# Where the constants lie: the fp32 identity behind the others, and kT tiles rounded up to 128 bytes

## The chip, the cores and the metric

The kernel runs on one core of a Trainium2 chip. The metric is the device time of one execution in microseconds, the lower the better. A kernel's time is the median of its runs; the profile comes from one further execution.

## The reference, cut to what matters

```python
# q, k, v: (8, 8, 576, 64) fp32;  w_in: (512, 2048);  w_out: (2048, 512)
scores = q @ k.T / 8                       # per batch and head, 576 x 576
rel = pos[:, None] - pos[None, :]
mask_local   = (rel >= 0) & (rel < 32)                 # heads 0 to 3
mask_strided = (rel >= 0) & (pos % 32 equal)           # heads 4 to 7
attn = softmax(where(mask, scores, -1e9))
x = (attn @ v) laid out as (4608 tokens, 512)
h = x @ w_in
out = where(h > 0, h, exp(min(h, 0)) - 1) @ w_out      # (4608, 512) fp32
```

So it is a sparse attention (a band of 32 keys for half of the heads, every 32nd key for the other half), followed by a two-layer network with an ELU between the layers.

## The kernel before

All data of a batch are brought in by DMAs that POOL issues and that turn fp32 into bf16 on the way. Strided heads are laid out so that partition p holds eight neighbouring positions, local heads in blocks of 96 or 128 positions. The attention of a batch works on four pairs of heads ("s0", "s1" strided, "l0", "l1" local), each in two halves: scores on PE (`scores`, L457), exponentials on ACT (`exp_s`, L464), the mask on DVE (`mask`, L471 and L477), the product with v on PE (`pv`, L484 to L527), then log, exponential and a product on ACT and DVE that put the normalised result into `xT`. The network works on nine chunks of 512 tokens: `l1` (L612) makes 16 groups of 128 hidden units, `exp_h`, `clamp` and `elu` (L620 to L640) apply the ELU and write the result into `g`, `l2` (L646) multiplies by `w_out_sb`, a copy (L652) brings the result into `osb`, and `store` (L664) writes it to HBM. The last group is cut into pieces (L676, L686).

The order of everything is written out by hand in one long list, ORDER, which every engine follows in its own queue: `w` is a matmul on zeros that only keeps PE going, `T` and `c` transpose q and k on PE and copy them out, `D` issues a load, `X` a DMA transpose, `S e m O n r x` are the steps of the attention and `a b L h i j g Z q o t` those of the network. Batches 0 and 1 are transposed on PE; from batch 2 on `dma_T` (L605) has SP's queue transpose the raw tiles into `qT` and `kT`. Loads to the raw tiles `qs`, `ks`, `vs` are runs of 512 bf16; `load_qloc` (L244), `load_kloc` (L251) and `load_vloc` (L261, L263) write pieces of 64 bf16, since two heads are woven into one row or a row of ones stands between two pieces of v. The weights come in eight loads, four to `w_in_sb` (L276) and four to `w_out_sb` (L280).

All tiles that live through the whole kernel come from one pool, `consts`, which lays them one behind another in the order in which they are named, each at the next multiple of 32 bytes of a partition. The order is: xT, g0, g1, w_in_sb, w_out_sb, zero, identity, identity_f, ones, the raw tiles qs, ks, ql, kl, vs, ql1, kl1, then vl0, vl1, vsp, the four qT, the four kT (s0, l0, s1, l1), and dist, same, eq, mask_s, mask_1, mask_l. Behind them come the pools of e, pm, ln, he, he1 and osb. `identity_f` is the fp32 identity with which the first q and k, staged in `g[0]` as fp32, are transposed (L405); it is written by one memset on DVE (L307) and one select on POOL (L312). Batch 1 is loaded into parts of xT and g[1] instead of the raw tiles.

```python
identity = consts.tile([128, 128], BF16, tag="identity", name="identity")
identity_f = consts.tile([RS, RS], F32, tag="identity_f", name="identity_f")   # RS = 72
ones = consts.tile([128, D], BF16, tag="ones", name="ones")
KSW = 2 * NS * RP + 128 - RP       # 1328 bf16 = 2656 bytes
KLW = PRE + 2 * S                  # 1184 bf16 = 2368 bytes
```

Of the kernel before, what the change touches and what calls it, by code (L numbers as in the profile page):

```python
# [8 lines left out]
F32 = mybir.dt.float32  # L9
BF16 = mybir.dt.bfloat16  # L10
# [6 lines left out]
D = 64  # L17
HG = 4
NS = 8
RS = S // NS  # L20
RP = 80
LQ = 96
LB = S // LQ
LN = LQ // NS
PRE = STRIDE
# [124 lines left out]
def kernel(  # L150
# [18 lines left out]
    consts = ctx.enter_context(tc.tile_pool(name="consts", bufs=1))  # L169
# [13 lines left out]
    w_out_sb = consts.tile([128, MC, d_model], BF16, tag="w_out_sb", name="w_out_sb")  # L183
    zero = consts.tile([128, CHUNK], BF16, tag="zero", name="zero")
    identity = consts.tile([128, 128], BF16, tag="identity", name="identity")
    identity_f = consts.tile([RS, RS], F32, tag="identity_f", name="identity_f")
    ones = consts.tile([128, D], BF16, tag="ones", name="ones")


# [17 lines left out]
    KLW = PRE + 2 * S  # L207

    qT = [{c: consts.tile([128, 2 * NS * RP], BF16, tag=f"qT{c}{i}", name=f"qT{c}{i}")
           for c in "sl"} for i in range(2)]  # L210
    kT = [{c: consts.tile([128, n], BF16, tag=f"kT{c}{i}", name=f"kT{c}{i}")
           for c, n in (("s", KSW), ("l", KLW))} for i in range(2)]
    dist = consts.tile([RS, RS], I32, tag="dist", name="dist")
    same = consts.tile([RS, RS], I32, tag="same", name="same")
# [1 line left out]
    mask_s = consts.tile([RS, RS], BF16, tag="mask_s", name="mask_s")  # L216
    mask_1 = consts.tile([128, NS, LN], BF16, tag="mask_1", name="mask_1")
    mask_l = consts.tile([128, 2, NS, 3, LN], BF16, tag="mask_l", name="mask_l")

    def rawof(nm, b):  # L220
        if b == 1:
            return raw1[nm]
        return odd[nm] if b % 2 and nm in odd else raw[nm]

    def runs(x, b, h, n):

        rows = RP if (b * H + h + n - 1) * S + RP * NS <= B * H * S else RS
        return rows, bass.AP(x.tensor, x.offset + (b * H + h) * S * D,
                             [[NS * D, rows], [S * D, n], [1, NS * D]])
# [65 lines left out]
    for eng, n, x in ((nc.sync, 0, q), (nc.scalar, 1, k)):  # L295
        for i in range(2):
            rows, in_ = runs(x, 0, HG, 2)
            f = NS * D // 2
            eng.dma_start(out=half(stage[0:rows, n * 4 * f:(n + 1) * 4 * f], i),
                          in_=in_[:, :, i * f:(i + 1) * f])  # L300
# [12 lines left out]
        identity_f, identity_f, compare_op=ALU.is_equal, fill=0.0,  # L313
# [281 lines left out]
    def dma_T(what, b):  # L595
        nm, c = what
        n = HG * NS // 2
        t = (qT if nm == "q" else kT)[int(b) % 2][c]
        in_ = rawof(what, int(b))
        if what == "kl":  # L600
            t, in_ = t[:, PRE:], in_[:, 0:HG * LB * D]
        else:
            t = t[:, 0:n * RP]
        p = LQ if what == "kl" else RP
        nc.sync.dma_start_transpose(out=t.rearrange("c (n p) -> c n p", p=p), in_=in_)  # L605
# [75 lines left out]
    def out_piece(ch, kk, i):  # L681
# [11 lines left out]
        "C": lambda *a: copy_T(nc.scalar.copy, *a),  # L693
        "S": scores, "e": exp_s, "m": mask, "O": pv, "n": log_sums, "r": recip, "x": write_x,
        "V": copy_vloc, "W": copy_vstr, "D": load, "X": dma_T,
        "a": lambda ch, m, bk: l1(ch, m, (2, 3), bk), "b": lambda ch, m: l1(ch, m, (0, 1)),
        "L": lambda ch, m, bk: l1(ch, m, (2, 3, 0, 1), bk), "h": exp_h,
# [39 lines left out]
```

## Time and profile before

| | |
|---|---|
| median of 3 runs | 307.03 us (306.18 to 308.11) |
| profiled execution | 306.21 us, of which the span is 304.5 us |
| PE busy (matmul) | 297.1 us, 98% |
| ACT, DVE, POOL busy | 226.8, 225.5, 81.0 us |
| DMA packets | 107,358, 37.63 MB |
| POOL's DMA queue (q0) | 69,728 packets, 19.47 MB, 72.0% of 16 engines |
| HBM read, written | 39.53 MB, 9.44 MB |

A busy share is that of an engine's instructions; DMA-issuing instructions are not counted. Matmuls are pipelined and their ends are modelled, so the groups' mean durations (379 ns for a matmul of 512 columns) are longer than the distance from one start to the next. The share of a DMA queue adds up the times of its packets over 16 engines; packets in flight at the same time count twice, so it can be over 100% of a stretch.

### The profile page before, as it was taken

What the parts mean: (1) busy time and instruction counts of PE and PEld (TensorE: products, weight loads), DVE (VectorE), ACT (ScalarE), POOL (GpSimd) and SP (SyncE); (2) the same over time, 40 slices, a digit from 0 to 9 for tenths busy, and PEclk for the clock granted to TensorE, in tenths of its full rate; (3) what the DMA queues carried; (4) which work ended last, traced back from release to release, by engine and by line L of the source; (5) the groups of instructions that cost most, each with busy time, mean ns of one, the idle gap of its engine ahead of it and who ended that gap; (6) DMA issues with size and microseconds to landing.
All of it is one profiled execution on the core that took longest, in us unless ns stands there. A gap on an engine that the chain in (4) does not pass through costs nothing.

```text
span 304.5 us, 6251 instructions
## 1 busy us (share of the span) xinstructions
PE 297.1 (98%) x2336; PEld 147.1 (48%) x2336; DVE 225.5 (74%) x435; ACT 226.8 (74%) x409; POOL 81.0 (27%) x111
## 2 busy tenths in 40 slices
PE   7999999999999999999999999999999999999994
PEld 3654455445544454445544554445444544444444
DVE  6777868698789978896788878976788358895020
ACT  2878778598879888997989889978777569982101
POOL 8823436651085008521087350000000000000000
PEclk9999999999999999999999999999999999999999
DMA  7999999999999999999989999931120022000054
GB/s 164 178 205 207 206 193 158 142 184 171 201 137 139 195 155 143 142 185 161 194 145 159 62 144 110 209 72 56 38 69 0 2 69 69 2 1 0 4 152 123
DMA packets 107358, 37.63 MB, mean 124 GB/s; under 512 B 89152, under 2 KB 102848, under 8 KB 107328
## 3 DMA queue, kind: packets, MB, share of 16 engines
q0 software_dynamic: 69728, 19.47, 72.0%
q1 hardware_dynamic: 36920, 17.08, 30.8%
q10 hardware_dynamic: 680, 0.69, 0.8%
q8 instruction: 18, 0.29, 0.4%
q14 instruction: 12, 0.10, 0.1%
HBM read 39.53 MB, written 9.44 MB: 161 GB/s over the span
## 4 chain that ended last, share of the span: by engine, by line
PE 82%; DMA 13%; DVE 2%; POOL 1%; issue 1%; ACTq 0%; DVEq 0%
PE ps L646 38%; PE ps L612 35%; DMA w_out_sb<-in_moe_w_out_dram 6%; DMA w_in_sb<-in_moe_w_in_dram 5%; PE ps L457 3%; PE ps L527 2%; PE ps L520 2%; DMA g<-in_k_dram 2%; PE ps L676 1%; DVE g L640 1%; POOL w_in_sb L276 1%; POOL vl L261 0%; DVE he L629 0%; DVE xT L585 0%; POOL xT L234 0%
## 5 line engine op out<-in xcount | busy, mean ns | idle before, releaser
L646 PE MATMUL ps<-w_out_sb,g 128*128 128x512 bf16 x560 | 132.8, 379 | 1.0 <-DVE g L640 0.5
L612 PE MATMUL ps<-xT,w_in_sb 128*128 128x512 bf16 x576 | 130.5, 379 | 0.1
L620 ACT ACTIVATE he<-ps 128x512 f32<-128x512 f32 x144 | 80.9, 597 | 22.0 <-PE ps L612 20.1
L612 PEld LDWEIGHTS <-w_in_sb 128*128 128x128 bf16 x576 | 54.9, 98 | 64.4 <-issue 1.2
L646 PEld LDWEIGHTS <-g 128*128 128x128 bf16 x560 | 51.2, 97 | 56.2 <-issue 1.1
L640 DVE TENSOR_TENSOR g<-he,ps 128x512 bf16<-128x512 bf16 x92 | 62.0, 684 | 1.9
L585 DVE TENSOR_TENSOR xT<-ps,ln 64x576 bf16<-64x576 f32 (+1 forms) x64 | 42.6, 678 | 20.1 <-ACT ln L560 19.1
L464 ACT ACTIVATE e<-ps 72x576 bf16<-72x576 f32 (+1 forms) x64 | 39.1, 647 | 15.6 <-PE ps L457 14.5
L629 DVE TENSOR_SCALAR he<-he 128x512 bf16<-128x512 f32 x92 | 39.2, 435 | 7.8 <-ACT he L620 7.4
L555 ACT ACTIVATE ln<-ps 64x576 f32<-64x576 f32 (+1 forms) x64 | 36.2, 583 | 10.0 <-PE ps L527 4.9
L638 DVE SCALAR_TENSOR_TENSOR g<-he,ps 128x512 bf16<-128x512 bf16 x52 | 34.8, 683 | 7.2 <-ACT he L627 6.7
L560 ACT ACTIVATE ln<-ln 64x576 f32<-64x576 f32 (+1 forms) x64 | 38.5, 619 | 1.2
L627 ACT ACTIVATE he<-he 128x512 bf16<-128x512 f32 x52 | 32.5, 630 | 1.0 <-DVE g L640 0.6
L652 DVE COPY osb<-ps 128x512 f32<-128x512 f32 x22 | 15.1, 685 | 16.8 <-PE ps L646 16.5
L244 POOL DMA_DIRECT2D ql<-in_q_dram x24 | 20.4, 855 | 10.5 <-DMA vl<-in_v_dram 5.7
L251 POOL DMA_DIRECT2D kl<-in_k_dram x24 | 17.9, 751 | 15.2 <-DMA w_out_sb<-in_moe_w_out_dram 4.5
L652 ACT COPY osb<-ps 128x512 f32<-128x512 f32 x13 | 7.6, 586 | 17.9 <-PE ps L646 14.1
L477 DVE TENSOR_TENSOR pm<-e,mask_l 128x576 bf16<-128x576 bf16 x32 | 14.1, 454 | 7.0 <-ACT e L464 5.4
L471 DVE TENSOR_TENSOR pm<-e,mask_s 72x576 bf16<-72x576 bf16 x32 | 14.2, 450 | 4.4 <-ACT e L464 4.2
L520 PEld LDWEIGHTS <-vsp 72*128 72x128 bf16 x192 | 9.1, 98 | 5.5 <-DVE pm L471 0.3
L261 POOL DMA_DIRECT2D vl<-in_v_dram x8 | 9.8, 1230 | 7.1 <-PE ps L527 4.9
L234 POOL DMA_DIRECT2D vs<-in_v_dram x8 | 5.2, 650 | 21.1 <-DVE vsp L592 17.8
(90 smaller groups left out, 152.2 us busy)
## 6 DMA issues: line engine op xcount, KB each, us to landing
out_dram<-osb SPq DMA_DIRECT2D x30, 144.0 KB
vl<-in_v_dram POOLq DMA_DIRECT2D x8, 288.0 KB, 9.9
w_in_sb<-in_moe_w_in_dram POOLq DMA_DIRECT2D x4, 512.0 KB, 13.7
w_out_sb<-in_moe_w_out_dram POOLq DMA_DIRECT2D x4, 512.0 KB, 17.4
kl<-in_k_dram POOLq DMA_DIRECT2D x24, 72.0 KB, 8.6
ql<-in_q_dram POOLq DMA_DIRECT2D x24, 72.0 KB, 8.5
ks<-in_k_dram POOLq DMA_DIRECT2D x5, 320.0 KB, 9.2
vs<-in_v_dram POOLq DMA_DIRECT2D x5, 320.0 KB, 9.6
```

Of the source, the lines that this page charges most:

```text
L464: nc.scalar.activation(e[0:R], tiles.pop(("S", key, u))[0:R], ACT.Exp, scale=scale)
L555: nc.scalar.activation(t, s_ps, ACT.Ln)
L560: nc.scalar.activation(t, t, ACT.Exp, scale=-1.0)
L585: nc.vector.tensor_mul(dst, o_ps, rc)
L612: nc.tensor.matmul(tiles["h", ch, m], lhsT=w_in_sb[:, c, m * 128:(m + 1) * 128], rhs=xT[:, c, ch * CHUNK:(ch + 1) * CHUNK], start=(c == 2) ...
L620: nc.scalar.activation(e, tiles["h", i[0], i[1]], ACT.Exp)
L627: nc.scalar.activation(e1, e, ACT.Relu, bias=1.0, scale=-1.0)
L629: eng.tensor_scalar(e1, e, scalar1=1.0, scalar2=1.0, op0=ALU.min, op1=ALU.subtract)
L638: nc.vector.scalar_tensor_tensor(dst, e1, -1.0, h, op0=ALU.mult, op1=ALU.max)
L640: nc.vector.tensor_tensor(dst, e1, h, op=ALU.max)
L646: nc.tensor.matmul(ops, lhsT=g[ch % 2][:, m, kk * 128:(kk + 1) * 128], rhs=w_out_sb[:, m, :], start=(m == 0), stop=(m == MC - 1), skip_gro ...
L652: eng(o_sb, tiles.pop(("o", int(ch), int(kk))))
```

## The change

identity_f is allocated last instead of between identity and ones, with a row of 80 instead of 72 fp32 (320 instead of 288 bytes), of which the first 72 are used. The kT tiles are rounded up to a multiple of 64 bf16: 1344 instead of 1328 (2688 bytes) and 1216 instead of 1184 (2432 bytes). The transpose into kTl names its end, KLW, since the tile is now longer. With that, ones and all tiles that DMAs write start at multiples of 128 bytes. No instruction is added, removed or moved; two clears of kTs are 8 words longer.

```diff
     identity = consts.tile([128, 128], BF16, tag="identity", name="identity")
-    identity_f = consts.tile([RS, RS], F32, tag="identity_f", name="identity_f")
     ones = consts.tile([128, D], BF16, tag="ones", name="ones")
...
-    kT = [{c: consts.tile([128, n], BF16, tag=f"kT{c}{i}", name=f"kT{c}{i}")
+    kT = [{c: consts.tile([128, -(-n // 64) * 64], BF16, tag=f"kT{c}{i}", name=f"kT{c}{i}")
            for c, n in (("s", KSW), ("l", KLW))} for i in range(2)]
...
     mask_l = consts.tile([128, 2, NS, 3, LN], BF16, tag="mask_l", name="mask_l")
+    identity_f = consts.tile([RS, RP], F32, tag="identity_f", name="identity_f")[:, 0:RS]
...
         if what == "kl":
-            t, in_ = t[:, PRE:], in_[:, 0:HG * LB * D]
+            t, in_ = t[:, PRE:KLW], in_[:, 0:HG * LB * D]
```

## The prediction

> **What bounds the kernel now.** I read the page first: which engine fills the span, how full the DMA engines are, and what the throttle grants.
>
> ```profile
> span 304.5 us, 6251 instructions
> ...
> PE 297.1 (98%) x2336; PEld 147.1 (48%) x2336; DVE 225.5 (74%) x435; ACT 226.8 (74%) x409; POOL 81.0 (27%) x111
> ...
> PEclk9999999999999999999999999999999999999999
> DMA  7999999999999999999989999931120022000054
> ...
> q0 software_dynamic: 69728, 19.47, 72.0%
> ```
>
> Two resources look full. PE is busy 98% of the span at full granted clock, and the DMA engines are busy in nine tenths or more of nearly every slice up to slice 24, which ends at 183 us (24 x 7.6). The change can only act on the second one directly, so the question is whether PE ever waits for it. I therefore cut the span into stages and read PE's idle time in each (length minus PE busy).
>
> ```profile
> core 0: us, PE busy (x) PEld busy (x) DVE busy (x) ACT busy (x) POOL busy (x), PEclk, DMA share, GB/s
> 0.00:18.50 18.50, 16.10 (x256) 9.65 (x256) 13.62 (x49) 10.68 (x23) 13.65 (x26) 1.00 1.18 177
> 18.50:45.00 26.50, 25.95 (x250) 13.19 (x245) 19.37 (x37) 19.41 (x38) 8.97 (x12) 1.00 1.32 203
> 45.00:94.90 49.90, 49.80 (x409) 24.37 (x409) 41.51 (x80) 40.42 (x78) 22.17 (x29) 1.00 1.68 161
> 94.90:102.20 7.30, 6.83 (x52) 3.19 (x51) 7.23 (x14) 6.52 (x12) 3.32 (x4) 1.00 1.85 170
> 102.20:297.00 194.80, 194.76 (x1329) 93.47 (x1329) 143.18 (x256) 148.78 (x260) 32.88 (x41) 1.00 0.82 96
> 297.00:304.50 7.50, 3.60 (x49) 3.24 (x47) 0.58 (x2) 0.96 (x2) 0.00 (x0) 0.98 0.41 120
> ```
>
> PE's idle time is 2.40, 0.55, 0.10, 0.47, 0.04 and 3.90 us, 7.46 in all. The first has the launch in it and the last the final copies and stores; between 18.5 and 297 us only 1.16 us are idle. The next view, what PE waited for, says how much of that is a transfer.
>
> ```profile
> PE ps L391 <- DVE zero L305: 1.3, 1, 1.3
> PE ps L405 <- DMA g<-in_k_dram: 0.5, 1, 0.5
> PE ps L646 <- DVE g L640: 0.5, 1, 0.5
> PE ps L646 <- DMA w_out_sb<-in_moe_w_out_dram: 0.5, 1, 0.5
> PE ps L500 <- issue: 0.4, 1, 0.4
> PE ps L411 <- DMA ks<-in_k_dram: 0.2, 1, 0.2
> ```
>
> Three waits are for DMAs, 1.2 us together. One is for the staged fp32 rows in g, one for w_out_sb, one for ks. So the kernel is bound by PE's own instruction stream; the full DMA engines run ahead of it. The chain in order of time shows the one place after the start where the two meet:
>
> ```profile
> 27.95 17.07 DMA w_out_sb<-in_moe_w_out_dram
> 45.07 1.89 PE ps L646 x8
> ```
>
> The last quarter of w_out is issued at 27.95, lands 17.07 us later, and PE starts on it at 45.07. Anything that moves this landing later costs its full length; anything that moves it earlier gains at most the wait of 0.5 us, since the work behind it is PE's own.
>
> **The change part by part.** The orders of instructions on all engines are the same; only addresses move. Before, identity_f is 72 fp32 = 288 bytes a partition, 2 x 128 + 32, so everything behind it lies at 32 mod 128: the raw q, k, v tiles, vl, qT, e, pm, he and osb. The kT tiles are 2656 and 2368 bytes, which puts kTs0, kTl0, kTs1 and kTl1 at 32, 0, 64 and 32. After, all of these start at multiples of 128. xT, g, w_in_sb and w_out_sb stand ahead of identity_f and do not move.
>
> Long runs into the raw tiles. I compare a stretch in which the writes go to tiles at 32 mod 128 (4 to 9 us: qs, ks, ql, kl, vs) with one in which they go to tiles that are aligned already (23 to 29 us: w_out_sb, xT, g). Columns: packets, MB, and their time as a share of 16 engines; a share over 100% means that packets overlap.
>
> ```profile
> q0 software_dynamic: 897, 0.85, 107.3%
> ...
> q0 software_dynamic: 1238, 1.23, 123.9%
> ```
>
> A packet takes 1.073 x 16 x 5000 / 897 = 95.7 ns in the first and 1.239 x 16 x 6000 / 1238 = 96.1 ns in the second. Packets of about 1 KB cost the same on both kinds of address, so I cost these loads, and the ks wait of 0.2 us with them, at no change.
>
> Short runs. ql and kl from batch 2 on, and all of vl, are written in pieces of 64 bf16 = 128 bytes (24 x 72 x 8 + 24 x 96 x 6 + 8 x 96 x 24 + 6 x 32 x 23 = 50,496 of the 69,728 packets). Every one of these starts at 32 mod 128 before, so the trace has no aligned row to compare with. The nearest rows are a stretch nearly full of them (162 to 166 us) and the aligned one above:
>
> ```profile
> q0 software_dynamic: 3246, 0.61, 241.6%
> ```
>
> Here each engine finishes a packet per 4000 x 16 / 3246 = 19.7 ns; the aligned 1 KB packets go at 6000 x 16 / 1238 = 77.5 ns, or 9.7 ns for 128 bytes. So alignment gains between nothing (the 1 KB rows show none) and 10 ns a packet, at most 50,496 x 10 / 16 = 31.6 us of transfer time over the whole kernel. Nearly all of it is off the path: PE waits for no ql, kl or vl at all. On the path lies what stands ahead of w_out's landing: the first vl load of 96 x 24 = 2304 packets, at most 2304 x 10 / 16 = 1.4 us, and that gain is cut off at the wait of 0.5 us. Below nothing the bound is also small: a packet that got 1 ns slower would cost 0.14 us there. I take 0.3 us gained, over half of the wait, because the short runs are the only packets whose alignment could matter and even a fifth of the upper bound gives it.
>
> The Trainium skill ("DMA: Bandwidth & Descriptors", Specifications) speaks against even that: below 512 bytes a transfer is done as read-modify-write, whatever its address, and the pieces keep their 128 bytes. By that rule the gain is 0 and the forecast below would be 307.0; the price of 19.7 against 9.7 ns agrees with a toll on short runs, and no row here separates length from address.
>
> Transposes and stores. The 24 transposes read the raw tiles and write qT and kT, and the stores read osb, all on SP's queue. They may get cheaper too, but PE waits for none of them, and the first is issued when w_out has landed:
>
> ```profile
> L605 SPq DMA_TRANSPOSE kTs<-ks x6: 1511/1780/4124, 48.3 to 178.7; - x6
> ```
>
> I cost them at nothing. The cover is PE's own work, with 0.04 us idle in the 194.8 us from 102.2 on; if PE had to wait for them, a us later would cost a us. The tail is PE's last copy and the store behind it:
>
> ```profile
> 300.64 0.29 DVE L686 COPY osb<-ps 128x128 f32<-128x128 f32 x1 [0.60 <-PE ps L676]
> ```
>
> 3.5 us pass from its end to the end of the span for two small stores; their length in packets doesn't change, so I leave it.
>
> What is added. The two kTs clears grow from 60 to 68 words:
>
> ```profile
> L334 DVE MEMSET kTs<- 128x60 uint32 x2 | 0.2, 108 | 0.0
> ```
>
> At most 8/60 of 108 ns, 14 ns each, in a stage in which DVE is busy 13.62 of 18.5 us: nothing.
>
> Compute on moved tiles. This is what could cost more than a transfer. I look for instructions of one engine and size whose operands lie at both kinds of address before:
>
> ```profile
> L640 DVE TENSOR_TENSOR g<-he,ps 128x512 bf16<-128x512 bf16 x92 | 62.0, 684 | 1.9
> L652 DVE COPY osb<-ps 128x512 f32<-128x512 f32 x22 | 15.1, 685 | 16.8 <-PE ps L646 16.5
> ...
> L612 PEld LDWEIGHTS <-w_in_sb 128*128 128x128 bf16 x576 | 54.9, 98 | 64.4 <-issue 1.2
> L520 PEld LDWEIGHTS <-vsp 72*128 72x128 bf16 x192 | 9.1, 98 | 5.5 <-DVE pm L471 0.3 <-issue 0.3
> L457 PEld LDWEIGHTS <-kTs 64*128 64x128 bf16 x240 | 4.7, 96 | 5.8 <-issue 5.7
> ```
>
> DVE takes 684 ns to write aligned g and 685 to write osb at 32 mod 128; a weight load takes 98 ns from aligned w_in_sb, 98 from vsp and 96 from kTs. Engines do not feel these offsets, so no gain and no loss there.
>
> The sum, against the profiled execution: 306.21 - 0.3 = 305.9. The median of the three runs, 307.03, is 0.82 above it, so the forecast for a median is 306.7 us.
>
> **The rivals.** A, compute gets slower. Engine operands could now collide because most tiles share the same start mod 128 (or faster transfers hit the banks that DVE reads). DVE is the engine nearest to PE: in the stage 94.9 to 102.2 it is busy 7.23 of 7.30 us, and in these stretches of 20 us
>
> ```profile
> 60.00:80.00 20.00, 19.98 (x172) 9.67 (x170) 18.09 (x35) 17.40 (x32) 5.37 (x7) 1.00 1.63 179
> 120.00:140.00 20.00, 20.00 (x145) 9.61 (x144) 18.51 (x34) 18.03 (x34) 9.01 (x12) 1.00 1.84 155
> 180.00:200.00 20.00, 20.00 (x125) 9.45 (x124) 18.38 (x34) 17.94 (x33) 0.00 (x0) 1.00 1.36 159
> ```
>
> it is over 90% full. With DVE 20% slower they overrun by 18.09 x 1.2 - 20 = 1.7, 2.2 and 2.1 us, and the short stage by 7.23 x 0.2 = 1.4: 7.4 us, 314.1. It decides (over 3 us) from about 13%: 0.4 + 0.9 + 0.8 + 0.9 = 3.0. Against it stand the equal rows above, but they test one operand at a time and never two tiles that agree mod 128. The Trainium skill ("SBUF — State Buffer", SBUF: two separate sides) is against it as well: DMA and engine ports are said not to contend.
>
> B, PE's score blocks get cheaper. After a block of score matmuls (L457) the next group runs longer:
>
> ```profile
> 74.46 0.86 PE ps L646 x4
> ...
> 77.32 0.36 PE ps L457 x12
> 77.68 0.97 PE ps L646 x4
> ...
> 105.69 0.36 PE ps L457 x12
> 106.06 1.83 PE ps L646 x8
> ```
>
> 0.97 against 0.86 for four; if that 0.1 us came from kT's address, some 32 blocks of two score calls would give 32 x 0.1 = 3.2 us back, 303.5. Against it: by the order of the program the block at 77 us reads batch 2's kTl0, aligned before, the one at 105 us batch 3's kTl1, at 32 mod 128, and both take 0.36 and leave the same 0.1 (8 x 0.216 = 1.73). So I think it belongs to switching between 64 and 128 rows.
>
> C, w_out lands later. If short loads behind it get faster they take a larger part of the shared engines. w_out's 17.07 us grow by perhaps 5%, 0.9 us, all of it on the path: 307.03 + 0.9 = 307.9.
>
> D, no effect at all: 307.0. The same case as the forecast for every purpose but 0.3 us.
>
> **How the numbers follow.** Forecast with D 0.66, C 0.08, A and other costs of compute on moved tiles 0.18, B or another gain in PE's stream 0.08. About 1% (3.1 us) is what a measurement of this kernel tells from no change; the forecast, C and D lie within it, A beyond it above, B beyond it below. So faster 0.08, same 0.74, slower 0.18. The likeliest case has its own range of 305.5 to 307.9: 307.03 minus all 1.2 us of DMA waits and a little, to C. To hold 8 in 10 I stretch it to 304.8 (half of B) and 309.6 (A at 13%).
>
> **What would show it right or wrong.** Right: q0's share falls below 72.0% if short runs get cheaper, or stays if the rule holds; PE's wait for w_out shrinks from 0.5 us and PE busy stays at 297 us. Wrong: PE busy or the mean of L640, L620 or L457 changes (A or B), or the wait for w_out grows (C). The whole forecast fails if PE's idle time between 18.5 and 297 us grows by over 2 us.

## The result, and the profile after

| | before | after |
|---|---|---|
| median | 306.63 us (18 runs, 306.04 to 308.11) | 305.88 us (18 runs, 305.40 to 306.82) |
| ratio | | 0.9973, 95% interval 0.9961 to 0.9985 |
| profiled execution | 306.21 us, span 304.5 | 306.14 us, span 304.4 |

The change gains about 0.8 us (0.27% of 306.6; by the interval 0.5 to 1.2 us). The two profiled executions differ by only 0.07 us, so they can show what became cheaper, but not by themselves where the 0.8 us are: a median says more here than a pair of traces.

These are the lines of after's page that answer to those of before:

```profile
span 304.4 us, 6211 instructions
...
PE 295.2 (97%) x2296; PEld 147.7 (49%) x2336; DVE 226.3 (74%) x435; ACT 226.7 (74%) x409; POOL 80.4 (26%) x111
...
DMA  8999999999999959999899499701120022000053
...
q0 software_dynamic: 69728, 19.47, 62.4%
```

The trace of after lacks 40 records of matmuls (x2296, against x2336 weight loads), so its 295.2 us are too low and say nothing of a faster PE. What has changed is q0: the same 69,728 packets and the same bytes take 62.4% of 16 engines instead of 72.0%. The DMA digits now show gaps before slice 24, where before there were nearly none. The same stages as in the prediction show it in the share of the DMA engines (the column after the clock):

```profile
0.00:18.50 18.50, 17.02 (x256) 10.51 (x258) 14.03 (x49) 10.84 (x24) 14.05 (x27) 1.00 1.18 181
...
45.00:94.90 49.90, 49.20 (x404) 24.38 (x411) 42.21 (x81) 40.88 (x78) 24.03 (x31) 1.00 1.56 170
94.90:102.20 7.30, 6.78 (x52) 3.28 (x52) 7.13 (x14) 6.56 (x12) 0.49 (x1) 1.00 1.72 160
102.20:297.00 194.80, 192.82 (x1304) 93.52 (x1330) 143.02 (x256) 148.60 (x260) 33.03 (x41) 1.00 0.67 94
```

From 102.2 us on, where the short runs of q, k and v are nearly the only loads, it falls from 0.82 to 0.67; in the first 18.5 us it stays at 1.18. DVE and ACT work as long as before. What PE waited for, in after:

```profile
PE ps L391 <- DVE zero L305: 1.3, 1, 1.3
PE ps L646 <- DVE g L640: 0.7, 2, 0.5
PE ps L646 <- issue: 0.6, 4, 0.2
PE ps L612 <- issue: 0.3, 2, 0.2
PE ps L391 <- issue: 0.2, 1, 0.2
```

All three waits for DMAs (g, w_out_sb and ks, 1.2 us together) are gone. Whether that was the gain is a question for experiments, since such waits differ between executions of one kernel: a second execution of the kernel before has only 0.3 us of them (below).

### The profile page after: what moved, and what is told of

It reads as the page before. It is cut to its first block, busy times and chain, and to the rows that moved or that the text cites. A ratio compares the mean times of both kernels' runs of the same rounds, so it can differ in the third digit from the quotient of the medians.

```text
span 304.4 us, 6211 instructions
## 1 busy us (share of the span) xinstructions
PE 295.2 (97%) x2296; PEld 147.7 (49%) x2336; DVE 226.3 (74%) x435; ACT 226.7 (74%) x409; POOL 80.4 (26%) x111
## 3 DMA queue, kind: packets, MB, share of 16 engines
q0 software_dynamic: 69728, 19.47, 62.4%
## 4 chain that ended last, share of the span: by engine, by line
PE 85%; DVE 7%; ACT 3%; issue 3%; ACTq 0%
PE ps L646 38%; PE ps L612 33%; PE ps L457 3%; DVE g L640 3%; PE ps L391 2%; DVE he L629 2%; PE ps L527 2%; PE ps L520 2%; ACT he L620 1%; PE ps L676 1%; ACT ln L555 1%; PE ps L414 1%; DVE g L638 1%; ACT ln L560 1%; PE ps L484 1%
## 5 line engine op out<-in xcount | busy, mean ns | idle before, releaser
L646 PE MATMUL ps<-w_out_sb,g 128*128 128x512 bf16 x538 | 129.6, 379 | 2.2 <-DVE g L640 0.7
L612 PE MATMUL ps<-xT,w_in_sb 128*128 128x512 bf16 x559 | 129.2, 379 | 1.4 <-issue 0.3
L620 ACT ACTIVATE he<-ps 128x512 f32<-128x512 f32 x144 | 80.9, 596 | 22.3 <-PE ps L612 18.9
L612 PEld LDWEIGHTS <-w_in_sb 128*128 128x128 bf16 x576 | 55.0, 98 | 64.4 <-issue 1.3
L629 DVE TENSOR_SCALAR he<-he 128x512 bf16<-128x512 f32 x92 | 39.9, 443 | 7.4 <-ACT he L620 6.6
L477 DVE TENSOR_TENSOR pm<-e,mask_l 128x576 bf16<-128x576 bf16 x32 | 14.1, 454 | 6.8 <-ACT e L464 5.3
## 6 DMA issues: line engine op xcount, KB each, us to landing
w_in_sb<-in_moe_w_in_dram POOLq DMA_DIRECT2D x4, 512.0 KB, 13.1
w_out_sb<-in_moe_w_out_dram POOLq DMA_DIRECT2D x4, 512.0 KB, 16.9
```

The costliest lines, as they stand in the source:

```text
L612: nc.tensor.matmul(tiles["h", ch, m], lhsT=w_in_sb[:, c, m * 128:(m + 1) * 128], rhs=xT[:, c, ch * CHUNK:(ch + 1) * CHUNK], start=(c == 2) ...
L620: nc.scalar.activation(e, tiles["h", i[0], i[1]], ACT.Exp)
L629: eng.tensor_scalar(e1, e, scalar1=1.0, scalar2=1.0, op0=ALU.min, op1=ALU.subtract)
L646: nc.tensor.matmul(ops, lhsT=g[ch % 2][:, m, kk * 128:(kk + 1) * 128], rhs=w_out_sb[:, m, :], start=(m == 0), stop=(m == MC - 1), skip_gro ...
```

## The experiments

Ratios are against runs of the kernel before on the same chip, with 95% intervals (12 runs of each kernel against 35 of before, except the loads alone). Padding tiles only move addresses; no instruction changes. A padded kernel's line numbers are 2 higher (L591 is L589, L614 is L612).

### Does before differ from itself?

> The kernel before, once more, for the spread of its profile. Theory 1 (short writes at 32 mod 128 are dearer in busy stretches, and the early loads land later for it): q0's share again 70 to 74%, PE's waits for DMAs again 0.8 to 1.5 us in all. Rival (the share of 72.0 against 62.4% is chance of one execution): the share falls anywhere from 62 to 72%. Time: both 1.000 of before.

Unchanged, it gave 1.0009 (0.9987 to 1.0031), with q0 at 71.8%, as expected. So the lower share in after is no chance of one execution. With 12 runs an interval reaches about 0.002 to either side, and a ratio whose interval holds 1 can't be told from no change. One expectation failed: PE's waits for DMAs came to 0.3 us (L405 for g) instead of 0.8 to 1.5, and there was none for w_out_sb. The wait of 0.5 us on which the forecast rested is thus not in every execution of the kernel before.

### Which tiles carry the gain?

```diff
 # raw_vl_only: before, with
+    pad0 = consts.tile([128, 48], BF16, tag="pad0", name="pad0")     # behind ones
+    pad1 = consts.tile([128, 16], BF16, tag="pad1", name="pad1")     # behind vs_p
 # rest_only: after, with the same two pads of 16 and 48
```

> Only the tiles that POOL's loads write (raw q, k, v and vl, with vsp) are put at 0 mod 128 by a pad of 96 bytes; a pad of 32 behind vsp leaves qT, kT, e, pm, he and osb where the kernel before has them. Theory 1: all of the gain, q0's share 61 to 65%, time 0.997 of before. Rival (the transposes' destinations, or osb that the stores read, or the engines' operands make the gain): share 70 to 74%, time 1.000.

> The complement: qT, kT, e, pm, he and osb as in the changed kernel, at 0 mod 128, but raw q, k, v, vl and vsp left at 32. Theory 1: none of the gain, q0's share 70 to 74%, time 1.000 of before. Rival (qT, kT or osb): share 62 to 66%, time 0.997.

raw_vl_only (only the raw tiles, vl and vsp aligned) gave 0.9972 (0.9956 to 0.9989), the whole gain. rest_only (everything else aligned: qT, kT, e, pm, he, osb) gave 0.9999 (0.9980 to 1.0018), nothing. The pages agree, raw_vl_only first:

```profile
q0 software_dynamic: 69728, 19.47, 63.7%
```

```profile
q0 software_dynamic: 69728, 19.47, 71.1%
```

So the rounding of kT, the place of osb and the clears do nothing that can be measured here. Next, the two groups apart:

```diff
 # raw_only: before, with
+    pad0 = consts.tile([128, 48], BF16, tag="pad0", name="pad0")     # behind ones
+    pad1 = consts.tile([128, 16], BF16, tag="pad1", name="pad1")     # ahead of vl
 # vl_only: before, with pads of 48 ahead of vl and 16 behind vs_p
```

> Only the raw q, k, v tiles at 0 mod 128; vl, vsp and all behind them as before (32, qT 32). The early loads of ql and kl are long runs, the short ones come from 37 us on. Theory 1a (PE gains where the first vl load, 2304 short pieces at 7 us, lands sooner: DVE's copy L589 waits for it, and masks and PE behind that): q0's share 66 to 69% but time 0.999 to 1.000, the copy starts at 15.6 us or later as before. Rival 1b (the later short loads of ql and kl make the gain): time 0.997 to 0.998.

> Only vl and vsp at 0 mod 128; raw tiles at 32 as before. Theory 1a: q0's share 66 to 69%, time 0.997 to 0.998, the copy L589 starts at 15.3 to 15.5 us. Rival 1b: time 0.999 to 1.000.

raw_only gave 0.9986 (0.9968 to 1.0004), vl_only 0.9980 (0.9963 to 0.9996); q0 stood at 64.8% and 64.9%, below the 66 to 69% expected. raw_only can't be told from no change by its interval, and its ratio is in neither of the two ranges expected. The intervals are too wide to order the two. DVE's copy started at 15.45 us in raw_only and at 15.79 in vl_only, the other way round from what was expected. The two also do not separate what they were meant to. raw_only's pads of 96 and 32 bytes move vl by 128 bytes in all, so it is unmoved counted by 128, but not counted by 256, and that is what turns out to matter below: in both kernels no piece of the first vl load crosses a multiple of 256.

### Is it w_out's wait, or the first vl load?

```diff
 # wo3_half: the last quarter of w_out loads two of four groups
+            if i == 3:
+                nc.gpsimd.dma_start(out=w_out_sb[:, 12:14, :], in_=w_out_v[:, 12:14, :])
+                return
-                rhs=w_out_sb[:, m, :], ...
+                rhs=w_out_sb[:, min(m, 13), :], ...
 # vl0_half: the first vl load brings 12 of 24 blocks, DVE clears the rest
+        if b == 0:
+            nc.gpsimd.dma_start(out=t[PRE:128, 0:12], in_=x[:, 0:12])
+            return
```

> The kernel before, but the last quarter of w_out is loaded by half (256 instead of 512 KB); the products that need the other half take the loaded part again, so PE's work is the same and that part of the result isn't the reference's. Its landing comes some 1.3 us earlier, before PE wants it. Theory 1 in its sharp form (the gain is the wait for w_out): the wait of 0.5 us goes, time 0.9975 to 0.9985 of before, q0's share 71 to 73%. Rival (the gain lies elsewhere, behind 45 us): time 0.9995 to 1.0005 although the wait is gone, because a later wait takes its place.

> The kernel before with its addresses, but the first vl load brings 12 of the 24 pieces a partition; the other 12 are cleared by a short DVE memset in idle time, so heads 2 and 3 of batch 0 get zeros for v. The load has 1152 short pieces less and lands about 1 us sooner. Theory 1a: the copy L589 no longer waits, first L612 0.3 to 0.6 us earlier than 18.5 us, time 0.997 to 0.9985 of before without any alignment, q0's share 70 to 72%. Rival 1b: time 0.9995 to 1.0005.

wo3_half takes the wait away on which the forecast rested, and gave 0.9996 (0.9976 to 1.0015): nothing. vl0_half touches no address and halves one load of 2,304 pieces; it gave 0.9968 (0.9952 to 0.9984), as much as the whole change. So the time of that first vl load matters. One path leads from it through DVE: its copy of the first vl (L589) waits for the load, and the masks (L477) and so PE stand behind the copy. Two traces show that chain closed, those of rest_only and at64 (further down). This is rest_only's, in order of time (start, us, what):

```profile
7.10 9.11 DMA vl<-in_v_dram
...
16.24 0.04 DVE vl L591
16.28 0.54 issue
16.82 0.47 DVE pm L479
...
21.31 1.89 PE ps L614 x8
```

and PE waits for the copy itself, by the view of its waits in rest_only:

```profile
PE ps L507 <- DVE vl L591: 0.5, 1, 0.5
```

In after the same stretch of the chain has no DMA in it, and the first full group of eight l1 matmuls on it starts 0.70 us earlier. That is the largest difference: in the timelines of before and before_again this group starts at 20.81 and 20.77, only 0.2 us later than in after.

```profile
16.05 0.46 PE ps L500 x2
...
20.61 1.89 PE ps L612 x8
```

In the timeline, before's copy sat idle for that load, after's didn't (start, length, then in brackets the idle time ahead of it); before first:

```profile
15.69 0.55 DVE L589 COPY vl<-vl 32x1472 bf16<-32x1472 bf16 x1 [0.30 <-DMA vl<-in_v_dram]
```

```profile
15.42 0.66 DVE L589 COPY vl<-vl 32x1472 bf16<-32x1472 bf16 x1
```

The landing of this one load, from issue on, is in the view of the tile vl up to 14 us (for before, up to 30 us); before, then after:

```profile
DMA to landing us min/median/max: 8.4/8.4/8.4
```

```profile
DMA to landing us min/median/max: 7.7/7.7/7.7
```

By the same view it took 8.3 in before_again and wo3_half and 9.1 in rest_only, which gained nothing, and 8.0 in raw_vl_only, 7.6 in raw_only, 7.1 in vl_only and 6.2 in vl0_half, whose ratios are all below 1 (raw_only's interval just reaches it).

The copy alone does not explain the gain. In vl0_half it starts at 15.81, no earlier than in before, and the first L612 at 18.56 instead of the expected 0.3 to 0.6 us ahead of before's 18.53; before_again's copy does not wait at all. A second path from the same load is in every trace: POOL issues the next load, a part of batch 1's q, only when the first vl has landed, and all later loads stand behind it in POOL's queue. In POOL's timeline, before first, then after:

```profile
15.95 0.65 POOL L234 DMA_DIRECT2D xT<-in_q_dram  x1 [1.49 <-DMA vl<-in_v_dram]
```

```profile
15.08 0.65 POOL L234 DMA_DIRECT2D xT<-in_q_dram  x1 [0.62 <-DMA vl<-in_v_dram]
```

This issue comes at 15.88 to 16.50 us in the five kernels that gained nothing (before, before_again, rest_only, wo3_half, at64) and at 14.44 to 15.51 in the five others. The runs' times differ in the same way: 40 of the 136 runs of the first five (88 of them of before, in three rounds) took 307 us or more, and 1 of the 66 of the others. So part of the gain is that long executions become rare, which a pair of traces hardly shows.

### Is a multiple of 64 enough?

```diff
 # at64: after, with
+    pad0 = consts.tile([128, 32], BF16, tag="pad0", name="pad0")     # behind ones
+    pad1 = consts.tile([128, 32], BF16, tag="pad1", name="pad1")     # behind vs_p
```

> The changed kernel with raw q, k, v, vl and vsp at 64 mod 128 instead of 0. If pieces of 128 bytes only have to start at a multiple of 64: q0's share 61 to 65% and time 0.997 of before, as with 0. If they have to start at a multiple of 128: share 69 to 74%, time 0.999 to 1.000.

No: 1.0010 (0.9991 to 1.0029), q0 at 71.3%, the first vl load 8.6 us to landing and again at the head of the chain (7.49 to 16.05 us). Its profiled execution took 308.05 us and so is one of the long ones. It has another wait that the prediction had excluded, PE waiting for a DMA transpose:

```profile
PE ps L459 <- DMA qTl<-ql: 0.8, 1, 0.8
PE ps L413 <- DMA ks<-in_k_dram: 0.7, 1, 0.7
```

This transpose is issued at 66.57 us, against 64.63 in before and 63.68 in after, and the stores behind it on SP's queue come later too. One of them holds up DVE's copy by 1.95 us, on the chain that ended last:

```profile
71.11 8.71 DMA out_dram<-osb
...
79.94 0.69 DVE osb L654
```

So here is a place where late loads cost time far behind the start. That the other long executions lose their time there too is not shown, since only this one was profiled.

### The price of the address alone

```diff
 # nothing but 24 loads of vl's form into 24 tiles, then a cast of each and stores of zeros
+    pad1 = consts.tile([128, OFF // 2], BF16, ...)          # OFF = 0, 32, 64
+    vl = [consts.tile([128, WD], BF16, ...) for i in range(24)]      # 6,272 bytes each
+        nc.gpsimd.dma_start(out=t[0:LQ], in_=x)             # 2,304 pieces of 128 bytes
```

> Only 24 loads in vl's form (55,296 pieces of 128 bytes) into 24 tiles at 0 mod 128, and at the end stores of zeros; all else is left out. If the toll on 32 mod 128 is in every piece: the loads take 47 to 52 us here and 60 to 70 at 32. If it arises only where queues mix: the same time in all three.

> The same loads into tiles at 32 mod 128. Toll in every piece: 60 to 70 us for the loads, mean packet over 40 ns. Toll only where queues mix: as at 0, mean packet 31 to 33 ns.

> The same loads into tiles at 64 mod 128. Lines of 64 bytes: as at 0. Lines of 128: as at 32.

The times were 77.85, 83.14 and 83.38 us (two runs each); the last landing comes at 50.6, 53.6 and 54.4 us. At 32 that is less than the 60 to 70 us expected for a toll in every piece. q0 on the pages of loads_at0, loads_at32 and loads_at64:

```profile
q0 software_dynamic: 55680, 7.08, 144.9%
```

```profile
q0 software_dynamic: 55680, 7.08, 188.9%
```

```profile
q0 software_dynamic: 55680, 7.08, 189.6%
```

A packet takes 1.449 x 76.5 x 16 / 55,680 = 31.9 ns in the first, and by the same sum 44.0 ns and 44.6 ns in the others. The surprise is in the landings, which the casts on DVE mark. In loads_at0's timeline, from the second to the last:

```profile
9.18 0.15 DVE L65 CAST osb<-vl 96x1 f32<-96x1 bf16 x1 [2.38 <-DMA vl<-in_q_dram]
...
50.59 0.15 DVE L65 CAST osb<-vl 96x1 f32<-96x1 bf16 x1 [1.72 <-DMA vl<-in_v_dram]
```

That is (50.59 - 9.18) / 22 = 1.88 us a load, evenly. In loads_at32 they alternate:

```profile
11.18 0.15 DVE L65 CAST osb<-vl 96x1 f32<-96x1 bf16 x1 [2.52 <-DMA vl<-in_q_dram]
12.69 0.15 DVE L65 CAST osb<-vl 96x1 f32<-96x1 bf16 x1 [1.35 <-DMA vl<-in_q_dram]
15.31 0.15 DVE L65 CAST osb<-vl 96x1 f32<-96x1 bf16 x1 [2.48 <-DMA vl<-in_q_dram]
16.82 0.15 DVE L65 CAST osb<-vl 96x1 f32<-96x1 bf16 x1 [1.35 <-DMA vl<-in_q_dram]
```

A tile of 6,272 bytes is 24.5 times 256, so here the tiles stand by turns at 32 and 160 beyond a multiple of 256, and their pieces, which begin 128 bytes into the tile, run from 160 to 288 or from 32 to 160. The slow ones are the first kind, which lie on both sides of a multiple of 256. To test this, all tiles of a group were made to stand alike:

```diff
 # loads_cross: tiles of 6,400 bytes = 25 x 256
+    WD = 25 * 128
+    # eight tiles with pieces from 160 to 288, eight from 32 to 160, eight from 224 to 352 (mod 256)
```

> The kernel holds nothing but 24 loads of vl's form (2,304 pieces of 128 bytes each, POOL, fp32 cast to bf16) and 36 stores of zeros, as loads_at0 and loads_at32 do; its output is zeros. Each tile is 6,400 bytes wide, so that all tiles of a group stand alike to 256 bytes. Counted from a multiple of 256, the first eight loads write pieces from byte 160 to 288, over a multiple of 256; the next eight write from 32 to 160, at no multiple of 128 but inside one block of 256 bytes; the last eight write from 224 to 352, over a multiple of 256 again. The landings are read from the 24 casts of L67 on DVE. Theory (a 128-byte piece is slow where it lies on both sides of a multiple of 256): the first and last eight loads land about 2.4 to 2.7 us apart, as the slow ones of loads_at32 did; the middle eight land as loads_at0's, 1.87 us apart or less. Span about 83 us or more (loads_at32: 81.0 with half of the loads crossing; this kernel has two thirds). Rival 1 (every start that is no multiple of 128 costs alike, and the alternation in loads_at32 is only an order in which neighbouring loads share the engines): all three groups alike, about 2.06 us apart or alternating as in loads_at32. Rival 2 (the cost is one of the start at a multiple of 64 or 32): the last group, at 96 within 128, as the middle one.

The three groups in loads_cross's timeline, a first and a last landing of each (the second and eighth, the eleventh and fifteenth, the eighteenth and twenty-third load):

```profile
10.20 0.15 DVE L67 CAST osb<-vl 96x1 f32<-96x1 bf16 x1 [2.48 <-DMA vl<-in_q_dram]
...
26.27 0.15 DVE L67 CAST osb<-vl 96x1 f32<-96x1 bf16 x1 [2.44 <-DMA vl<-in_q_dram]
...
31.14 0.15 DVE L67 CAST osb<-vl 96x1 f32<-96x1 bf16 x1 [1.72 <-DMA vl<-in_k_dram]
...
38.68 0.15 DVE L67 CAST osb<-vl 96x1 f32<-96x1 bf16 x1 [1.72 <-DMA vl<-in_k_dram]
...
46.31 0.15 DVE L67 CAST osb<-vl 96x1 f32<-96x1 bf16 x1 [2.51 <-DMA vl<-in_v_dram]
...
59.88 0.15 DVE L67 CAST osb<-vl 96x1 f32<-96x1 bf16 x1 [2.59 <-DMA vl<-in_v_dram]
```

That is 16.07 / 6 = 2.68 us, 7.54 / 4 = 1.89 us and 13.57 / 5 = 2.71 us a load. The middle group starts at no multiple of 128 and is as fast as the aligned loads. It and the first group stand alike counted by 128, 64 or 32, so both rivals named there fall. What costs is a piece that crosses a multiple of 256 bytes: 2.68 - 1.88 = 0.80 us for 2,304 pieces, or 5.6 ns of one of 16 engines for each. No view shows an address. That the slow groups are the crossing ones needs the pool to start 128 bytes beyond a multiple of 256; that is inferred from the order slow, fast, slow (with a start at a multiple of 256 the middle group would cross) and taken for the other kernels too. The Trainium skill ("DMA: Bandwidth & Descriptors", How a descriptor splits into AXI transactions) says that a descriptor is split at multiples of 256 bytes, so that a piece across one needs two transactions. The page speaks of reading; these runs, which write into SBUF, agree in kind and add the price.

Counted by the tiles' addresses, in before every piece of the even batches' vl and every second one of ql and kl crosses a multiple of 256: 4 x 2,304 + 3 x 736 + 27,648 / 2 = 25,248 of the 50,496 short pieces. At 64 (at64) the same half does. None crosses in after, raw_vl_only leaves none either, and rest_only leaves them all. raw_only leaves the odd batches' vl (11,424), vl_only half of ql and kl (13,824). So the first vl load crosses in before, rest_only, wo3_half, at64 and vl0_half, and not in after, raw_vl_only, raw_only and vl_only. It landed within 8.0 us in these last four and in vl0_half, which loads only half of it. A multiple of 128 is thus sufficient for pieces of 128 bytes, not necessary.

## Why the prediction was right or wrong, point by point

**The size and the sign.** The forecast of 306.7 us was 0.3 us below the median of three runs. With 18 runs before stands at 306.63, 0.40 below the figure the sum was set against, and the gain is 0.75 between the medians, not 0.3. Both shifts go the same way, so the result lies 0.82 us below the forecast, inside the range. That it lies inside is owed to the width of the range: the gain was forecast at less than half of its size, and on a path that did not carry it. The edges of the range do not come out quite as said, either: half of B's 3.2 us below 306.7 is 305.1 (304.8 stands there), A at 13% is 309.7 (309.6), and A and B are counted from 306.7, C and D from 307.03. The result lies inside either way.

**Long runs cost the same: held.** The two stretches of the prediction in after, 4 to 9 us and 23 to 29 us:

```profile
q0 software_dynamic: 897, 0.84, 104.2%
```

```profile
q0 software_dynamic: 1236, 1.23, 123.9%
```

That is 92.9 and 96.2 ns a packet, against 95.7 and 96.1: at most 3% for the moved tiles.

**Short runs gain 0 to 10 ns of an engine each: held, and in the middle.** The loads alone give 5.6 ns for a crossing piece and nothing for others, and so by estimate 0.80 us for the first vl load, where the bound was 1.4; in the kernel itself it landed 0.7 us sooner (8.4 to 7.7). In after, 162 to 166 us, an engine finishes a packet in 4000 x 16 / 4667 = 13.7 ns (before 19.7, with another mix of loads), close to the 1.88 x 16 / 2304 = 13.1 ns of the loads alone:

```profile
q0 software_dynamic: 4667, 0.60, 231.7%
```

**The rule weighed against the row: it did not decide.** The read-modify-write below 512 bytes of the Trainium skill ("DMA: Bandwidth & Descriptors", Specifications), which the page states without a word on the address, would by itself have left q0 at 72.0%. It fell to 62.4% with the lengths unchanged, so address has a price of its own; whether length has one too is not shown here.

**The step that failed: "PE waits for no ql, kl or vl at all", and with it the 0.3 us at w_out's landing.** The prediction looked at what PE waited for directly, found w_out, and stopped. DVE's wait of 0.30 us and POOL's of 1.49 us for the first vl load were in the trace, one engine further back: masks that PE needs stand behind the first, all later loads behind the second. wo3_half shows that w_out's 0.5 us are not where the time lies, and before_again does not have them at all; vl0_half shows that sparing one half of that vl load is worth as much as the whole change. "PE waits for none of them" was too strong for the transposes as well: at64 has 0.8 us at L459. The wait for w_out and the lack of one for the transposes were both read from one execution and taken for all.

**What stays open.** That crossing pieces in the tiles of POOL's loads make the gain is shown (raw_vl_only and rest_only for the tiles, the loads alone for the crossing). Where PE gets it back is not. vl0_half takes out 1,152 packets as well as crossings, which leaves room for all transfers of the start, and neither its copy nor its first L612 comes earlier than in before. In before's profiled execution, the chain that ended last went through w_in and w_out. So the first vl load is the likeliest origin, shown on the chain in rest_only and at64, but how much of the 0.8 us goes through DVE's copy, through the other waits of the start (ks, g) or through POOL's queue to later waits was not separated.

**Nothing from compute: held.** The groups in after:

```profile
L640 DVE TENSOR_TENSOR g<-he,ps 128x512 bf16<-128x512 bf16 x92 | 62.0, 684 | 1.9
...
L652 DVE COPY osb<-ps 128x512 f32<-128x512 f32 x22 | 15.1, 685 | 16.3 <-PE ps L646 16.0
...
L520 PEld LDWEIGHTS <-vsp 72*128 72x128 bf16 x192 | 9.1, 98 | 5.4 <-DVE pm L471 0.3 <-issue 0.3
...
L457 PEld LDWEIGHTS <-kTs 64*128 64x128 bf16 x240 | 4.7, 96 | 5.8 <-issue 5.2 <-DMA out_dram<-osb 0.4
...
L334 DVE MEMSET kTs<- 128x68 uint32 x2 | 0.2, 115 | 0.0
```

684, 685, 98 and 96 ns are those of before, the ACTIVATE of L620 has 596 ns (before 597), the matmuls of L457 have 196 to 204 (before 197 to 204), and the clears grew by 7 ns each. Rival A (compute slower) and B (cheaper score blocks) did not come about. C (w_out later) went the other way: its landing, as a median of four loads in the page's DMA issues, went from 17.4 to 16.9 us; before first:

```profile
w_out_sb<-in_moe_w_out_dram POOLq DMA_DIRECT2D x4, 512.0 KB, 17.4
```

```profile
w_out_sb<-in_moe_w_out_dram POOLq DMA_DIRECT2D x4, 512.0 KB, 16.9
```

## What to carry to other kernels

Where a DMA scatters short pieces into SBUF, place the tile so that no piece crosses a multiple of 256 bytes; tiles at multiples of 128 do it for pieces of 128 bytes, the only length tried here, and the addresses alone tell whether it is so. Expect little from it while PE sets the end: 9.6 points of a queue's share became 0.27% of the time here. Before saying that the bound engine does not wait for a transfer, follow the waits of the engines that feed it too, the one that issues the loads included, and read several executions.

## What the runs showed of the hardware that was not expected

A casting load of 2,304 pieces of 128 bytes takes 1.88 to 1.89 us in a row of such loads, aligned or not, and 2.68 to 2.71 us if the pieces cross a multiple of 256. When crossing and other loads alternate (loads_at32), two take 15.31 - 11.18 = 4.13 us together, 0.4 us less than 2.68 + 1.88; the cause was not tried. The stores at the end of these kernels moved as well, since osb lies behind the vl tiles: from the first issue to the last, the 36 of them take 21.52 us in loads_at0 and 23.74 to 23.75 in the three others. Which property of osb's address does it was not tried. So the times of these whole kernels hold more than the price of the loads, and the landings are the measure.
